# Wider value and state products in the first six chunks, and paired state updates later, in an mLSTM and feed-forward kernel

## The chip, the core and the metric

The kernel runs on one core of one Trainium2 chip. Five engines work side by side and wait for each other through semaphores: TensorE (PE, with its weight loads shown apart as PEld), VectorE (DVE), ScalarE (ACT), GpSimd (POOL) and SyncE (SP), which issues the transfers. The metric is the device time of one execution in microseconds, as the median of several runs. TensorE's clock has two levels, 1.2 and 2.4 GHz; the profile gives the granted one as a share of full speed (1.00 or 0.50).

## What is computed

Four sequences of 768 tokens with 8 heads of 40 channels go through a gated linear recurrence; the result goes through a feed-forward layer with 2048 hidden units. Cut to what matters:

```python
for t in range(S):
    m_new  = maximum(f[t] + m, i[t])
    f_stab = exp(f[t] + m - m_new); i_stab = exp(i[t] - m_new); m = m_new
    C = f_stab * C + i_stab * outer(v[t], k[t])
    n = f_stab * n + i_stab * k[t]
    y[t] = sigmoid(o[t]) * (C @ q[t]) / maximum(abs(n . q[t]), 1)
h = x @ w_in;  out = (maximum(h, 0) + alpha * minimum(h, 0)) @ w_out
```

## The kernel before

**Tiling.** A sequence is cut into 6 chunks of 128 tokens, which makes 24 chunks, numbered n = 0 to 23 over the four sequences; c is a chunk's number in its own sequence. Two chunks make a group of 256 tokens, g = 0 to 11. Inside a chunk the recurrence is done with products: scores `pS` of keys and queries, a decay matrix `E`, their product on DVE (L1082, or L346 later), and then values `pH`: per head the 128x128 matrix E as the stationary operand and the 42 columns of `va` (40 channels, two constants for the denominator) as the moving one. What older chunks left comes from the state C through `pI` (`from_state`). At a chunk's end the state is updated with a product `pu` of the weighed keys `kd` and `va` (`update_steps`); the last chunk of a sequence has no update.

**Two regimes.** The first six chunks (n < NDIR = 6) work with true float32 products (values in `values`, L313 to L326, one 42-column product for each of 8 heads; state in L381, one 84-column product for each of 4 pairs of heads). The trace shows each such float32 product as two matmuls. In that time the weights of the feed-forward layer are loaded and split into a high and a low part (the class `Weights`: ACT, DVE and POOL), which is why all engines are busy there. From n = 6 on all attention products are sums of bf16 parts, but for `pu`, which stays in float32.

**Feed-forward.** Each group runs 8 steps `up` (products `ph`, L742 to L749, 16 of 256 columns a step, in two PSUM banks in turn) and 8 steps `down` (products `po`, L779, 320 columns).

**Order.** The order of the program is a table: ORDER for the first two groups, PATTERN for each later one, in which `ua.0` and `ua.1` are the update products of a group's even and odd chunk. The instructions are pinned to it on each engine, so an instruction that waits holds up all that stand behind it on its engine.

**PSUM.** The attention products share four banks, in two pools "a" and "b" of two buffers, handed out in turn by `psa`.

**Fillers.** `dense` runs products of 256 bf16 columns whose result nobody reads. `values` puts 4, 14 and 4 of them ahead of the value products of chunks 3, 4 and 5 (FILL, L667).

Of the kernel before, what the change touches and what calls it, by code (L numbers as in the profile page):

```python
# [17 lines left out]
def kernel(ctx: ExitStack, tc: tile.TileContext, q, k, v, i_gate, f_gate, o_gate, w_in, w_out, alpha, out):  # L18
# [20 lines left out]
    ps_a = ctx.enter_context(tc.tile_pool(name="ps_a", bufs=2, space=bass.MemoryType.PSUM))  # L39
    turns = ["b", "a"]  # L40

    def psa(name):
        turns.reverse()
        return ps_a.tile([P, 512], F32, tag=turns[0], name=name)


    ident = const.tile([P, P], F32, tag="ident", name="ident")
# [105 lines left out]
        for _ in range(k):  # L153
            nc.tensor.matmul(dst[:, : 2 * P], x[:, :P], x, start=True, stop=True)  # L154

    kds = {}

    def weighed(n):

# [12 lines left out]
    def update_steps(n):  # L172
        b, c = divmod(n, NC)
        if c == NC - 1:
            return
        va = va_t[n // GC % NV][:, n % GC]
        if n not in kds:
            weighed(n)
        kd = kds.pop(n)
        pu = psa(f"pu{n}")  # L180
        pu3 = pu[:, : H * VA].rearrange("p (h e) -> p h e", e=VA)
        for h in range(H):
            r = slice(64 * (h % 2), 64 * (h % 2) + D)
            nc.tensor.matmul(pu3[r, h], kd[:, h], va[:, h], start=True, stop=True)  # L184
        yield
        if b > 0:
            yield from state(n, pu3)
            return
        old, new = C_t[(n - 1) % 3], C_t[n % 3]
        if c > 0 and n in CP:  # L190
            nc.gpsimd.tensor_tensor(
                new[:R], old[:R], gamB[:R, b * H : (b + 1) * H, c : c + 1].broadcast_to([R, H, VA]), ALU.mult
            )
        for par in range(2):
            r = slice(64 * par, 64 * par + D)
            to = by_parity(new[r], par)
            if c == 0:
                nc.vector.tensor_copy(to, by_parity(pu3[r], par))
            else:
                if n not in CP:  # L200
                    gam = gamB[r, b * H + par : (b + 1) * H : 2, c : c + 1].broadcast_to([D, NPR, VA])
                    nc.vector.tensor_tensor(to, by_parity(old[r], par), gam, ALU.mult)
                nc.vector.tensor_tensor(to, to, by_parity(pu3[r], par), ALU.add)
        yield

    def state(n, pu):

        b, c = divmod(n, NC)
        C = C_t[0][:D]
        if c > 0:  # L210
            nc.gpsimd.tensor_tensor(
                C, C, gamB[:D, b * H : (b + 1) * H, c : c + 1].broadcast_to([D, H, VA]), ALU.mult
            )
        yield
        for par in range(2):
            to, new = by_parity(C, par), by_parity(pu[64 * par : 64 * par + D], par)
            if c == 0:
                nc.vector.tensor_copy(to, new)
            else:
                nc.vector.tensor_tensor(to, to, new, ALU.add)  # L220
        yield
        X = state_parts(n)
        C = C.rearrange("p h e -> p (h e)")
        cw = sb.tile([P, 512], F32, tag="qf", name=f"cw{n}")
        rest, high = cw[:D, : H * VA], cw[:D, H * VA :].bitcast(BF16)[:, : H * VA]
        nc.scalar.copy(high, C)
        yield
        nc.gpsimd.tensor_tensor(rest, C, high, ALU.subtract)
        yield
        nc.scalar.copy(X[:D, 0], rest)  # L230
        yield
        nc.gpsimd.tensor_tensor(X[:D, 1], rest, X[:D, 0], ALU.subtract)
        yield
        nc.sync.dma_start(X[D : 2 * D, 0], high)
        nc.sync.dma_start(X[2 * D : 3 * D], high.unsqueeze(1).broadcast_to([D, 2, H * VA]))
        yield
        nc.sync.dma_start(X[D : 2 * D, 1], X[:D, 0])
        yield
# [71 lines left out]
            for _ in value_parts(n):  # L310
                pass

    def values(n, E, busy=lambda: None):  # L313

        pH = psa(f"pH{n}")
        dense(pH, FILL.get(n, 0))
        va = va_t[n // GC % NV][:, n % GC]
        for i in range(H):
            if i % 2 == 0:
                busy()  # L320
            par, p = divmod(i, NPR)
            h = 2 * p + par
            nc.tensor.matmul(  # L323
                pH[:, h * VA : (h + 1) * VA], E[par][:, p * P : (p + 1) * P], va[:, h], start=True, stop=True
            )
        return pH[:, : H * VA].rearrange("p (h e) -> p h e", e=VA)  # L326

# [26 lines left out]
    def values_by_parts(n, Es):  # L354

        V = vbs.pop(n)
        S = sb.tile([P, H, VA], F32, tag="T", name=f"S{n}")
        for par in range(2):
            pH = psa(f"pH{n}_{par}")
            for p in range(NPR):  # L360
                for k, e in enumerate(Es[par]):
                    nc.tensor.matmul(  # L362
                        pH[:, p * 3 * VA : (p * 3 + 3 - k) * VA], e[:, p * P : (p + 1) * P],
                        V[:, 2 * p + par, : 3 - k], start=k == 0, stop=k == 2,
                    )
            yield
            nc.vector.tensor_reduce(
                by_parity(S, par), pH[:, : NPR * 3 * VA].rearrange("p (r k e) -> p r e k", k=3, e=VA),
                mybir.AxisListType.X, ALU.add,
            )  # L370
            yield S

    def from_state(n, qf, Q=None):

        b, c = divmod(n, NC)
        pI = psa(f"pI{n}")
        if b == 0:
            C = C_t[(n - 1) % 3][:R].rearrange("p h e -> p (h e)")
            for p in range(NPR):
                es = slice(2 * p * VA, 2 * (p + 1) * VA)  # L380
                nc.tensor.matmul(pI[:, es], qf[:R, p * P : (p + 1) * P], C[:, es], start=True, stop=True)  # L381
        else:
            C = state_parts(n - 1)[: 3 * D]
            for h in range(H):
                es = slice(h * VA, (h + 1) * VA)
                for s in range(2):
                    nc.tensor.matmul(pI[:, es], Q[: 3 * D, s, h], C[:, s, es], start=s == 0, stop=s == 1)  # L387
        yield
        pI = pI[:, : H * VA].rearrange("p (h e) -> p h e", e=VA)

        T = sb.tile([P, H, VA], F32, tag="T", name=f"T{n}") if n < NBF else pI
        nc.vector.tensor_tensor(T, pI, eT[:, c, b * H : (b + 1) * H].unsqueeze(2).broadcast_to([P, H, VA]), ALU.mult)
        yield T
# [85 lines left out]
    def late_steps(n):  # L479
# [12 lines left out]

        def scores(par):
            Q, K, _ = chunk[n]
            pS[par] = psa(f"pS{n}_{par}")
            for p in range(NPR):
                h = 2 * p + par
                for s in range(2):
                    nc.tensor.matmul(  # L499
                        pS[par][:, p * P : (p + 1) * P], K[: 3 * D, s, h], Q[: 3 * D, s, h], start=s == 0, stop=s == 1  # L500
                    )
            got["s", par] = score_parts(pS[par], E[par], Es[par][2])
# [43 lines left out]
        if n > NDIR:  # L546
            st["sh"] = lambda: shifted(n)
            st["va"] = val
            for k in "bcd":
                st["v" + k] = nxt("v")  # L550
            if c < NC - 1:
                st["wd"] = lambda: weighed(n)
                st["ua"] = upd
                if c > 0:
                    st["ub"] = nxt("u")
                    st["uc"] = nxt("u")
                else:
                    st["uc"] = lambda: (next(got["u"]), next(got["u"]))
                for k in "defghi":
                    st["u" + k] = nxt("u")  # L560
# [79 lines left out]
    def first_stacks():  # L640
# [18 lines left out]
    OFF = 0  # L659
    NDIR = 6  # L660
    NBF = 6
    BEHIND = 4
    XNP = range(2, NBF)
    KDP = range(1, 24)
    CP = range(6, 24)
    OBA = range(0)
    FILL = {3: 4, 4: 14, 5: 4}  # L667
    ORDER = """warm18 kfz alT lf0z warm2 warm2 i00d i00s sca0 lf0a lf0b dq0 L0 sp01 qT0 dq1 alC li0 bj0 wt0 bTt kT0 i00x qc0 kc0 ewj
        i01d sca1 bTc ex01 sp00 sc00 qT1 wTt eeL wTc qc1 wd0 li1 lf1a lf1b kT1 sc01 i00j ex00 kc1 eTt Cz eTc sp11 ex11
        dv0 wg01 i01s wd1 L1 um0 uc0 i01x lpa um1 sp10 wg00 gma gmd ex10 i01j i00h fm1 ft1 sc11 do0 sc10 wg10 bj1 wtl  # L670
# [10 lines left out]
        U12 fm5 ft5 o5h sc51 wg51 v5 o7d R12 S12 ta5 D10 G11 K11 o6s o6x gr5 og3 gg5 G12 gx5 gg4 D11 K12 D12 i30h i30l  # L681
        gx4 U13 gp5 D02 tp0 do3 U06 o7s gp4 o5l o6j vp0 R13 tp1 g05 S13 G13 N05 K13 o7x o6h D13 vp1 o7j U07 tp2 tp3
        R06 S06 R07 x4 x5 xa5 xd5 D03 D04 D05 S07 o7h o7l G06 K06 o6l D06 xa4 xd4 G07 K07 D07 Z0"""
    PATTERN = """og.-1 ua.0 m1.0 V4<< tf.1 ub.0 vb.1 xn.-1 xp.-1 V5<< tg.1 g2<< m0.0 N2<< vc.1 c1.0 r4<< vb.0 d1.0 th.1 h1.0 ti.1 xw.-1 uc.0
        s4<< ud.0 D2<< ue.0 U6<< g4<< l1.0 g3<< N3<< uf.0 r5<< c0.0 vd.1 vc.0 ua.1 sh.1 X:-1 lG.-1 lG.2 ub.1 s5<< N4<<
        R6<< d0.0 g5<< ug.0 h0.0 l0.0 uc.1 V7<< N5<< vd.0 D3<< D4<< D5<< S6<< ta.2 tb.2 xa:-1 uh.0 lL.2
        y0.0 xd:-1 pi.0 r7<< s7<< G6<< wd.2 tc.2 K6<< q0.0 td.2 y1.0 F< q1.0 e0.1 te.2 V0< e1.1 oa.0 tf.2 g7<<
# [261 lines left out]
    def first_group():  # L949
# [38 lines left out]
            nc.vector.tensor_copy(pick[j * BH : (j + 1) * BH], ident[j * BH : (j + 1) * BH, j * BH : (j + 1) * BH])  # L988

        li = row_tile("g_li", "Lb", bufs=2)  # L990
        L = row_tile("g_L", "Lb", bufs=2)
        bj, wj, eL = f, rst, i

        def weights(c0, c1, engine):
# [32 lines left out]
        def spread(n, par):  # L1027

            pb = psa(f"pb{n}_{par}")
            barred(pb)  # L1030
            for p in range(NPR):
                h = 2 * p + par
                nc.tensor.matmul(
                    pb[:, p * P : (p + 1) * P], ident[:BH, h : h + 1].broadcast_to([BH, P]), L[:, n * P : (n + 1) * P],
                    start=False, stop=p == NPR - 1
                )
            rows[n, par] = pb
# [310 lines left out]
```

## Time and profile before

| | |
|---|---|
| median of 3 runs | 470.04 us (470.02 to 470.23) |
| the profiled execution | 470.16 us, of which the span is 468.4 us |
| PE busy | 461.9 us, 99% of the span |
| DVE, ACT, POOL busy | 334.1 us (71%), 316.1 us (67%), 308.4 us (66%) |
| granted TensorE clock | 1.00 but for a stretch of some 10 us from 24.3 us on, at 0.50 |
| PE idle in 40 us stretches from 140 to 420 us | 0.00 us |

The span begins with the first instruction and ends with the last; 1.8 us of the execution lie outside it. A matmul's end is modelled, and neighbours overlap, so a PE that is busy all the time can still be short of its best. How long PE takes for a piece of work is best read from the start of one row to the start of the next. A row of the timeline merges equal instructions that follow each other.

### The profile page before, as it was taken

To read this page: it belongs to the slowest core of one execution; us is meant where nothing else is said; L and a number is where in the kernel's file an instruction comes from. 1 tells how busy PE (TensorE), PEld (TensorE's weight loads), DVE (VectorE), ACT (ScalarE), POOL (GpSimd) and SP (SyncE) were. 2 spreads that over 40 slices of the span, in tenths; PEclk is the share of its full clock that TensorE was granted. 3 is DMA by queue.
4 is the path that set the end of the run, shared out by engine and by line. 5 is a ranking of instruction groups with operands and counts; after the bars stand their busy time and mean duration, and the time that the engine had idled before them with its cause. 6 is when DMAs were issued, how large, how long until landed. Compare 5 with 4: busy or idle time off the path is not lost.

```text
span 468.4 us, 11843 instructions
## 1 busy us (share of the span) xinstructions
PE 461.9 (99%) x4388; PEld 449.2 (96%) x4388; DVE 334.1 (71%) x691; ACT 316.1 (67%) x707; POOL 308.4 (66%) x377
## 2 busy tenths in 40 slices
PE   8999999999999999999999999999999999999996
PEld 6899989999999999999999999999999999999996
DVE  4768988766777887886787887887777886674321
ACT  4969988775857767767867867757857758524331
POOL 8531574864697787597697697587798696324231
PEclk9959999999999999999999999999999999999999
DMA  9988995887786676887996686789895453021000
GB/s 186 197 193 212 233 252 138 192 156 145 154 195 158 129 170 178 134 166 171 160 209 170 121 170 174 146 153 188 172 190 158 96 131 111 1 73 25 29 0 29
DMA packets 186306, 68.68 MB, mean 147 GB/s; under 512 B 150234, under 2 KB 178506, under 8 KB 186250
## 3 DMA queue, kind: packets, MB, share of 16 engines
q1 hardware_dynamic: 186170, 67.83, 66.4%
q8 instruction: 35, 0.57, 0.5%
q14 instruction: 21, 0.17, 0.1%
q10 hardware_dynamic: 80, 0.11, 0.1%
HBM read 40.44 MB, written 7.57 MB: 102 GB/s over the span
## 4 chain that ended last, share of the span: by engine, by line
PE 91%; DVE 5%; ACT 2%; issue 1%; POOL 0%; DVEq 0%; POOLq 0%; ACTq 0%
PE po L779 36%; PE ph L742 5%; PE ph L748 5%; PE ph L745 5%; PE ph L743 5%; PE ph L744 5%; PE ph L747 4%; PE ph L746 4%; PE ph L749 4%; PE pH L362 4%; PE pS L499 3%; PE pH L323 2%; PE pS L1078 2%; PE pu L184 2%; PE pI L387 1%; PE warm L154 1%
## 5 line engine op out<-in xcount | busy, mean ns | idle before, releaser
L768 POOL TENSOR_TENSOR gl<-g,gh 128x512 fp32r<-128x512 f32 x77 | 100.4, 1305 | 43.7 <-ACT gh L766 40.4
L779 PE MATMUL po<-OH,gh 128*128 128x320 f32 x368 | 110.7, 312 | 0.0
L779 PE MATMUL po<-OL,gh 128*128 128x320 f32 x368 | 109.3, 309 | 0.0
L752 ACT ACTIVATE g<-ph 128x512 f32<-128x512 f32 x96 | 57.1, 596 | 58.9 <-PE ph L749 57.7
L757 DVE SCALAR_TENSOR_TENSOR g<-g,oma,ph 128x256 f32<-128x256 f32 x156 | 66.7, 468 | 32.7 <-ACT g L752 32.3
L779 PEld LDWEIGHTS po<-OL,gh 128*128 128x128 f32 x368 | 69.2, 188 | 0.1
L779 PEld LDWEIGHTS po<-OH,gh 128*128 128x128 f32 x368 | 69.1, 188 | 0.0
L779 PE MATMUL po<-OH,gl 128*128 128x320 f32 x368 | 69.0, 309 | 0.0
L742 PE MATMUL ph<-XH,WH 128*128 128x256 f32 x192 | 57.7, 300 | 0.7 <-ACT wo L848 0.7
L779 PEld LDWEIGHTS po<-OH,gl 128*128 128x128 f32 x368 | 58.0, 188 | 0.0
L349 ACT CAST E<-pS 128x512 bf16<-128x512 f32 x72 | 41.7, 582 | 19.2 <-DVE pS L346 15.4
L748 PE MATMUL ph<-XL,WH 128*128 128x256 f32 x192 | 54.3, 283 | 0.0
L745 PE MATMUL ph<-XH,WL 128*128 128x256 f32 x192 | 54.3, 283 | 0.0
L747 PE MATMUL ph<-XL,WH 128*128 128x256 f32 x192 | 54.2, 282 | 0.0
L743 PE MATMUL ph<-XH,WH 128*128 128x256 f32 x192 | 54.1, 282 | 0.0
L744 PE MATMUL ph<-XH,WL 128*128 128x256 f32 x192 | 54.1, 282 | 0.0
L746 PE MATMUL ph<-XH,W 128*128 128x256 f32 x192 | 53.5, 278 | 0.2 <-POOL W L874 0.2
L749 PE MATMUL ph<-XL,W 128*128 128x256 f32 x192 | 53.4, 278 | 0.0
L766 ACT CAST gh<-g 128x512 fp32r<-128x512 f32 x77 | 46.5, 618 | 9.8 <-DVE g L757 7.4
L470 ACT ACTIVATE E<-Lb,bT 128x128 f32<-128x128 f32 x160 | 50.0, 392 | 0.0
L346 DVE TENSOR_TENSOR pS<-pS,E 128x512 f32<-128x512 f32 x36 | 24.7, 690 | 30.7 <-PE pS L499 23.5
L742 PEld LDWEIGHTS ph<-XH,WH 128*128 128x128 f32 x192 | 36.1, 188 | 1.9 <-ACT wo L848 0.9
(197 smaller groups left out, 1144.0 us busy)
## 6 DMA issues: line engine op xcount, KB each, us to landing
Lb<-L_d SPq DMA_DIRECT2D x20, 512.0 KB
wo<-in_moe_w_out_dram SPq DMA_DIRECT2D x8, 640.0 KB
wi<-in_moe_w_in_dram SPq DMA_DIRECT2D x8, 512.0 KB
qn<-in_q_dram SPq DMA_DIRECT2D x24, 160.0 KB
kn<-in_k_dram SPq DMA_DIRECT2D x24, 160.0 KB
va<-in_v_dram SPq DMA_DIRECT2D x24, 160.0 KB
og<-in_o_gate_dram SPq DMA_DIRECT2D x24, 160.0 KB
out_dram<-ob SPq DMA_DIRECT2D x11, 320.0 KB
```

The costliest lines, as they stand in the source:

```text
L742: nc.tensor.matmul(dst, WH[half][:, 0, hs], XH[:, 0], start=True, stop=False)
L743: nc.tensor.matmul(dst, WH[half][:, 1, hs], XH[:, 1], start=False, stop=False)
L744: nc.tensor.matmul(dst, WL[half][:, 0, hs], XH[:, 0], start=False, stop=False)
L745: nc.tensor.matmul(dst, WL[half][:, 1, hs], XH[:, 1], start=False, stop=False)
L746: nc.tensor.matmul(dst, W2[:, fs], X2, start=False, stop=False)
L747: nc.tensor.matmul(dst, WH[half][:, 0, hs], XL[:, 0], start=False, stop=False)
L748: nc.tensor.matmul(dst, WH[half][:, 1, hs], XL[:, 1], start=False, stop=False)
L749: nc.tensor.matmul(dst, W2[:, fs], X2L, start=False, stop=True)
L752: nc.scalar.activation(gt, ph, AF.Relu, scale=-1.0)
L757: nc.vector.scalar_tensor_tensor(out=y[:, e], in0=gt[:, e], scalar=oma[:, f : f + 1], in1=ph[:, e], op0=ALU.mult, op1=ALU.add)
L768: (nc.vector if split else nc.gpsimd).tensor_tensor(gl, y, gh.bitcast(F32), ALU.subtract)
L779: nc.tensor.matmul(po[j], x[:, e, j * P : (j + 1) * P], W[f // NB][:, f % NB], **ends)
```

## The change

Four things are changed.

1. In the first six chunks each value product has 126 columns (WIDE = 3 * VA) in place of 42: the moving operand repeats the head's 42 columns three times, and the result goes to columns that the next heads' products write over. Heads now follow each other as 0, 1, 2, ... in place of 0, 2, 4, 6, 1, 3, 5, 7, so the two E tiles alternate. The state products of chunks 1 to 5 have 126 columns in place of 84, but for the last of the four.
2. The fillers of chunks 3, 4 and 5 are gone.
3. The products that spread the row of decays for chunks 0 and 1 use all 128 rows in place of 32; the rows below are zero, from one more memset on DVE ahead of the first scan.
4. From chunk 7 on the update products of even and odd heads write the same columns in different partitions, so one chunk needs 168 columns of a bank in place of 336. The two chunks of a group then share one bank. From the fifth group on (g > 3) the odd chunk's update is done right behind the even one's (`uA.1` in PATTERN). Five groups have both updates and are moved: 4, 6, 7, 9 and 10. Late tiles get fixed pools: pS "a" and "b" by parity, pI "b", pH and pu "a".

On DVE, ACT, POOL and SP nothing moves; DVE has the memset more.

```diff
@@ psa and its tags
-    def psa(name):
-        turns.reverse()
-        return ps_a.tile([P, 512], F32, tag=turns[0], name=name)
+    def psa(name, tag=None):
+        if tag is None:
+            turns.reverse()
+            tag = turns[0]
+        return ps_a.tile([P, 512], F32, tag=tag, name=name)
+
+    def kept(n, tag, first):
+
+        return tag if n > first else None
...
+    def repeated(ps, at, w):
+
+        return ps[:, at : at + WIDE].rearrange("p (k w) -> p k w", w=w)
@@ update_steps
-        pu = psa(f"pu{n}")
-        pu3 = pu[:, : H * VA].rearrange("p (h e) -> p h e", e=VA)
+        late, j = n > NDIR, n % GC
+        if not late or j == 0 or n - 1 not in pus:
+            pu = psa(f"pu{n}", kept(n, "a", NDIR + 1))
+            if late and j == 0:
+                pus[n] = pu
+        else:
+            pu = pus.pop(n - 1)
+        if late:
+            pu3 = pu[:, j * NPR * VA : (j + 1) * NPR * VA].rearrange("p (r e) -> p r e", e=VA)
+        else:
+            pu3 = pu[:, : H * VA].rearrange("p (h e) -> p h e", e=VA)
         for h in range(H):
             r = slice(64 * (h % 2), 64 * (h % 2) + D)
-            nc.tensor.matmul(pu3[r, h], kd[:, h], va[:, h], start=True, stop=True)
+            nc.tensor.matmul(pu3[r, h // 2 if late else h], kd[:, h], va[:, h], start=True, stop=True)
@@ values
-    def values(n, E, busy=lambda: None):
+    def values(n, E):
 
         pH = psa(f"pH{n}")
-        dense(pH, FILL.get(n, 0))
         va = va_t[n // GC % NV][:, n % GC]
-        for i in range(H):
-            if i % 2 == 0:
-                busy()
-            par, p = divmod(i, NPR)
-            h = 2 * p + par
+        for h in range(H):
             nc.tensor.matmul(
-                pH[:, h * VA : (h + 1) * VA], E[par][:, p * P : (p + 1) * P], va[:, h], start=True, stop=True
+                repeated(pH, h * VA, VA), E[h % 2][:, h // 2 * P : (h // 2 + 1) * P],
+                va[:, h].unsqueeze(1).broadcast_to([P, WIDE // VA, VA]), start=True, stop=True,
             )
@@ from_state
                 es = slice(2 * p * VA, 2 * (p + 1) * VA)
+                es = slice(es.start, min(es.start + WIDE, H * VA))
@@ late_steps and the table
-                st["ua"] = upd
+                st["uA" if j and g > GF else "ua"] = upd
...
-    FILL = {3: 4, 4: 14, 5: 4}
+    WIDE = 3 * VA
...
-    PATTERN = """og.-1 ua.0 m1.0 ...
+    PATTERN = """og.-1 ua.0 uA.1 m1.0 ...
@@ first_group
-        L = row_tile("g_L", "Lb", bufs=2)
+        L_all = sb.tile([P, H, P], F32, tag="Lb", name="g_L", bufs=2).rearrange("p h t -> p (h t)")
+        nc.vector.memset(L_all[:, :GT], 0.0)
+        L = L_all[:BH, :S]
...
-                    pb[:, p * P : (p + 1) * P], ident[:BH, h : h + 1].broadcast_to([BH, P]), L[:, n * P : (n + 1) * P],
+                    pb[:, p * P : (p + 1) * P], ident[:, h : h + 1].broadcast_to([P, P]), L_all[:, n * P : (n + 1) * P],
```

**PE at the values of chunk 5, before.** pI is the state's share, pS_1 the scores of the odd heads, pH the values (first the fillers, four pairs of rows, then four even heads with E_0 and four odd ones with E_1), po the next `down` step.

```order
L381 MATMUL pI_1168<-C_86,qf_874 128x84 x4
L1078 MATMUL pS_1_1176<-qf_874,kf_133 128x128 x4
L154 LDWEIGHTS ident
L154 MATMUL pH_1182<-ident 128x256
...
L323 MATMUL pH_1182<-va_79,E_0_1106 128x42 x4
L323 MATMUL pH_1182<-va_79,E_1_1129 128x42 x4
L779 MATMUL po_0_1039<-OH_104,gg_0_1135 128x320
```

The same place after the change:

```order
L397 MATMUL pI_1151<-C_86,qf_871 128x126 x3
L397 MATMUL pI_1151<-C_86,qf_871 128x84
L1097 MATMUL pS_1_1159<-qf_871,kf_134 128x128 x4
L337 MATMUL pH_1165<-va_79,E_0_1089 128x126
L337 MATMUL pH_1165<-va_79,E_1_1112 128x126
...
L796 MATMUL po_0_1022<-OH_104,gg_0_1118 128x320
```

The fillers are gone, and the first product with E_1 now stands second of eight, not fifth.

**PE at the update products of group 4 (chunks 8 and 9), before.** pS_1 is the end of chunk 8's scores, the first pu row is chunk 8's update, ph_4 to ph_7 are `up` steps of an earlier group; three `up` steps and a `down` step lie between the two updates.

```order
L499 MATMUL pS_1_2045<-qS_1870,kS_1910 128x128
L184 MATMUL pu_2072<-va_79,kd_1717 40x42 x8
L742 MATMUL ph_4_2082<-XH_1418,WH_709 128x256
...
L749 MATMUL ph_6_2160<-XL_1419,W_73 128x256
L184 MATMUL pu_2191<-va_79,kd_1914 40x42 x8
L742 MATMUL ph_7_2224<-XH_1418,WH_709 128x256
```

The same place after the change:

```order
L515 MATMUL pS_1_2024<-qS_1849,kS_1889 128x128
L203 MATMUL pu_2051<-va_79,kd_1696 40x42 x8
L203 MATMUL pu_2051<-va_79,kd_1893 40x42 x8
L759 MATMUL ph_4_2069<-XH_1397,WH_710 128x256
...
L766 MATMUL ph_6_2147<-XL_1398,W_73 128x256
L759 MATMUL ph_7_2202<-XH_1397,WH_710 128x256
```

Chunk 9's eight update products moved up by 60 matmuls, into the bank of chunk 8's, and ph_7 follows ph_6 directly.

## Rows read from the trace of the kernel before

**Rows 1.** Stretches: length; busy us by engine; granted clock; DMA share; GB/s.

```profile
21.00:24.00 3.00, 3.00 (x27) 2.58 (x26) 2.88 (x8) 2.95 (x7) 1.56 (x3) 1.00 0.88 225
24.50:34.50 10.00, 10.00 (x51) 9.19 (x50) 7.01 (x14) 6.10 (x17) 2.35 (x3) 0.50 0.89 181
```

**Rows 2.** Timeline of PE, 18 to 50: start, us, line, out<-in, shapes.

```profile
18.95 1.99 PE L1078 MATMUL pS<-qf,kf 104*128 104x128 f32 x16
...
21.61 1.98 PE L323 MATMUL pH<-va,E 128*128 128x42 f32 x16
...
29.57 0.61 PE L94 MATMUL pb<-later,ident 128*128 128x512 bf16 x1
...
48.36 1.16 PE L1078 MATMUL pS<-qf,kf 104*128 104x128 f32 x8
```

**Rows 3.** Timelines of DVE, ACT, POOL and the SP queue, 27 to 37.

```profile
27.73 0.49 DVE L427 TENSOR_TENSOR xn<-pH,og 128x320 f32<-128x320 f32 x1
...
29.67 0.29 DVE L1007 COPY eT<-ps_ge 128x128 f32<-128x128 f32 x1 [1.45 <-PE ps_ge L1003]
...
32.52 0.69 DVE L1082 TENSOR_TENSOR E<-pS,E 128x512 f32<-128x512 f32 x1 [1.18 <-PE pS L1078]
...
35.39 0.69 DVE L1082 TENSOR_TENSOR E<-pS,E 128x512 f32<-128x512 f32 x1 [1.06 <-PE pS L1078]
...
30.64 1.14 ACT L1061 ACTIVATE E<-pb,bT 128x128 f32<-128x128 f32 x4 [2.82 <-PE pb L1045]
...
35.86 1.40 POOL L162 TENSOR_TENSOR kd<-kn,wT 128x320 f32<-128x320 f32 x2
...
36.60 0.37 SPq L100 DMA_DIRECT2D kn<-in_k_dram  x1
```

**Rows 4.** Stretches, the transfers: length, granted clock, DMA share, GB/s.

```profile
32.00:36.00 4.00, 0.68 0.02 4
...
38.00:52.00 14.00, 1.00 1.07 266
```

**Rows 5.** Chain that ended last, in order of time, 64 to 69.

```profile
64.06 0.81 ACT wo L848
...
68.15 1.53 PE pH L154 x14
```

**Rows 6.** Stretches with busy times, columns as in rows 1.

```profile
70.00:80.00 10.00, 9.98 (x109) 9.57 (x108) 9.58 (x23) 8.22 (x19) 4.45 (x5) 1.00 0.64 157
...
180.00:220.00 40.00, 40.00 (x409) 39.39 (x408) 30.02 (x60) 28.99 (x67) 30.61 (x37) 1.00 0.74 155
```

**Rows 7.** Timeline of PE and of DVE at the values of chunk 5.

```profile
81.14 0.60 PE L154 MATMUL pH<-ident 128*128 128x256 bf16 x4
81.58 1.88 PE L323 MATMUL pH<-va,E 128*128 128x42 f32 x16
83.29 0.39 PE L779 MATMUL po<-OH,gg 128*128 128x320 f32 x1
...
81.42 0.69 DVE L1082 TENSOR_TENSOR E<-pS,E 128x512 f32<-128x512 f32 x1 [0.79 <-POOL E L473]
```

**Rows 8.** Timeline of PE and DVE around updates: chunk 9's, then two together.

```profile
147.00 0.28 PE L749 MATMUL ph<-XL,W 128*128 128x256 f32 x1
147.20 0.51 PE L184 MATMUL pu<-va,kd 128*40 128x42 f32 x16
147.64 0.39 PE L742 MATMUL ph<-XH,WH 128*128 128x256 f32 x1
147.86 0.28 PE L743 MATMUL ph<-XH,WH 128*128 128x256 f32 x1
147.98 0.28 PE L744 MATMUL ph<-XH,WL 128*128 128x256 f32 x1
...
145.95 0.87 DVE L757 SCALAR_TENSOR_TENSOR g<-g,oma,ph 128x256 f32<-128x256 f32 x2 [1.60 <-ACT g L752]
...
73.29 0.81 PE L184 MATMUL pu<-va,kd 128*40 128x42 f32 x32
```

More of the change, by code (lines that the diff above doesn't have):

```diff
@@ L154, in dense @@
             nc.tensor.matmul(dst[:, : 2 * P], x[:, :P], x, start=True, stop=True)
-    kds = {}
+    def repeated(ps, at, w):
+        return ps[:, at : at + WIDE].rearrange("p (k w) -> p k w", w=w)
+    kds, pus = {}, {}
     def weighed(n):
@@ L179, in update_steps @@
         kd = kds.pop(n)
-        pu = psa(f"pu{n}")
-        pu3 = pu[:, : H * VA].rearrange("p (h e) -> p h e", e=VA)
+        late, j = n > NDIR, n % GC
[9 more added lines that the diff above has]
+            pu3 = pu[:, : H * VA].rearrange("p (h e) -> p h e", e=VA)
         for h in range(H):
             r = slice(64 * (h % 2), 64 * (h % 2) + D)
-            nc.tensor.matmul(pu3[r, h], kd[:, h], va[:, h], start=True, stop=True)
+            nc.tensor.matmul(pu3[r, h // 2 if late else h], kd[:, h], va[:, h], start=True, stop=True)
         yield
         if b > 0:
-            yield from state(n, pu3)
+            yield from state(n, [pu3[64 * par : 64 * par + D] if late else by_parity(pu3[64 * par : 64 * par + D], par) for par in range(2)])
             return
@@ L215, in state @@
         for par in range(2):
-            to, new = by_parity(C, par), by_parity(pu[64 * par : 64 * par + D], par)
+            to, new = by_parity(C, par), pu[par]
             if c == 0:
@@ L358, in values_by_parts @@
         for par in range(2):
-            pH = psa(f"pH{n}_{par}")
+            pH = psa(f"pH{n}_{par}", kept(n, "a", NDIR))
             for p in range(NPR):
@@ L375, in from_state @@
         b, c = divmod(n, NC)
-        pI = psa(f"pI{n}")
+        pI = psa(f"pI{n}", kept(n, "b", NDIR))
         if b == 0:
@@ L494, in scores @@
             Q, K, _ = chunk[n]
-            pS[par] = psa(f"pS{n}_{par}")
+            pS[par] = psa(f"pS{n}_{par}", kept(n, "ab"[par], NDIR + 1))
             for p in range(NPR):
@@ L661 @@
     NBF = 6
+    GF = NDIR // GC
     BEHIND = 4
@@ L683 @@
         R06 S06 R07 x4 x5 xa5 xd5 D03 D04 D05 S07 o7h o7l G06 K06 o6l D06 xa4 xd4 G07 K07 D07 Z0"""
-    PATTERN = """og.-1 ua.0 m1.0 V4<< tf.1 ub.0 vb.1 xn.-1 xp.-1 V5<< tg.1 g2<< m0.0 N2<< vc.1 c1.0 r4<< vb.0 d1.0 th.1 h1.0 ti.1 xw.-1 uc.0
+    PATTERN = """og.-1 ua.0 uA.1 m1.0 V4<< tf.1 ub.0 vb.1 xn.-1 xp.-1 V5<< tg.1 g2<< m0.0 N2<< vc.1 c1.0 r4<< vb.0 d1.0 th.1 h1.0 ti.1 xw.-1 uc.0
         s4<< ud.0 D2<< ue.0 U6<< g4<< l1.0 g3<< N3<< uf.0 r5<< c0.0 vd.1 vc.0 ua.1 sh.1 X:-1 lG.-1 lG.2 ub.1 s5<< N4<<
```

## The prediction

> **What bounds the kernel now.** I read the stretches first. From 140 us on PE is busy all the time and nobody makes it wait; the row of 180 to 220 stands for six such stretches [rows 6]. What PE does there is the time, so an instruction less on PE counts in full. The start is different: ACT and DVE convert the weights while the first chunks run, and the chain goes through them, as at 64.06 [rows 5]. And there is a stretch in which PE itself is slow: from about 24.5 to 34.5 us the granted clock is 0.50, which is the 1.2 GHz level, and before it 1.00 [rows 1]. PE never idled ahead of the fall: it was busy for 3.00 of 3.00 us. What it did was 16 matmuls of 42 columns, with transposes and some small products around them [rows 1, 2]. So I look for three things in the rows: what PE's slow stretch costs, which of the fillers lie on a path, and what an update product costs PE where PE is the bound.
>
> **The change part by part.**
>
> *The clock (part 1, and its cost).* At full clock 16 matmuls of 128 columns take 1.99 us and 16 of 42 columns 1.98 us [rows 2]: the moving columns are not what such a float32 product is paid for. So 126 columns cost between nothing and what the slowest case of 128 columns shows, 8 in 1.16 us, which is 2.32 for 16 against 1.98: up to 0.34 us a chunk [rows 2]. I take 0.1, since the direct comparison is nearest. The state products go from 84 to 126 columns; by the same rows that is nothing. Here a page speaks against the change. The Trainium skill, "TensorE: Matmul & The Clock Gate", section "Back-to-back issue gap", makes a stream of matmuls cost its columns; by it 84 more columns at 2.4 GHz are 35 ns a matmul, an estimate of 0.6 us a chunk, and 0.6 us later where a chunk's values end on the path. The rows disagree with it for these float32 products.
>
> For the clock itself I expect that it holds at 24.3: the stretch before the fall then has three times the moving columns in its 16 value matmuls, and the scores at 18.95, as wide as that, ran at full clock and kept it [rows 2]. PE's 10 us at half clock would be 5 us. How much of the other 5 arrives is a matter of who is late next. The first hold is the product at 29.57: it writes the bank of chunk 0's values, which DVE frees with xn, 27.73 + 0.49 = 28.22 [rows 2, 3]. So it starts at 28.3, 1.3 us earlier. From its start to ACT's exponentials are 1.07 us at half clock, 0.54 at full; the exponentials take 1.14, so DVE multiplies at 28.3 + 0.54 + 1.14 = 30.0 in place of 32.52: 2.5 us earlier [rows 2, 3]. DVE itself is in time for it: its small work from 29.67 to 31.34 (32.52 less the idle 1.18) is 1.67 us, its idle 1.45 ahead of that was for PE, so the work can run from 28.22 to 29.9. On this multiplication hang xn of chunk 1, the POOL work up to kd, and SP's load of kn at 36.60, which waits for kd: all 2.5 us earlier. From 32.52 to 35.39 DVE idles 1.06 for PE and works 1.81; with PE ahead the second multiplication comes at 30.0 + 1.8 = 31.8, 3.6 us earlier [rows 3]. So two offsets enter the conversion stage: 3.6 us for PE, DVE and ACT, 2.5 us for the loads. The loads matter: the transfer engines stand still from 32 to 36, because SP waits for kd, and are full from 38 to 52 [rows 3, 4]. No view shows how long a load lies ready before its use, so the stage comes out between 2.5 and 3.6 us earlier. I take 3.0, in the middle, with 2.4 to 3.8 as ends.
>
> *The fillers (part 2).* Chunk 4's fourteen are on the chain with 1.53 us [rows 5]. But DVE is busy for 9.58 of the next 10 us [rows 6], in its own order, so it takes up at most 0.42 us of that before it holds PE again. I take 0 and keep 0.4 for the range. Chunk 3's four stand inside the conversion stage and are covered by ACT and DVE there. Without this cover they would be worth a little over 0.4 us, as chunk 5's are. Chunk 5's four take 81.58 - 81.14 = 0.44 us of PE, and here the new order of heads bites. The values needed E of the odd heads from their fifth product on; now the second needs it. That E comes from DVE at 81.42 + 0.69 = 82.11, held by POOL [rows 7]. Now eight products run from 81.58 to 83.29, 0.214 us each. After the change the first runs at 81.14, PE then waits until 82.1, and seven more take 1.5 us, or 1.6 to 1.8 with the price of columns: the end is 83.6 to 83.9 against 83.29. So this place loses 0.3 to 0.6 us, and I take 0.4. Behind PE's wait stand the `down` products of group 1, which are PE's bound from there on.
>
> *The spread over 128 rows and the memset (part 3).* The same number of matmuls with the same columns. DVE's memset stands ahead of a scan that waits for the gates to arrive; that wait covers it. Were it not covered it would be one pass of DVE over 256 columns, about half of a 0.69 us row [rows 3]. I take 0.
>
> *The paired updates (part 4).* An update between two `up` steps: from the last ph before it (147.00) to the second ph behind it (147.86) are 0.86 us, where two ordinary steps are 2 x 0.12 = 0.24 (147.98 - 147.86 is one). So it costs 0.62 us. Two updates together are a row of 0.81 us, one is a row of 0.51, so the second costs 0.30 [rows 8]. Moving it saves 0.32 us, in five groups 1.6 us, all of it in the stretch where PE is the bound. What could take it back is the next step's bank: ph_7 needs DVE's work on ph_5, done at 145.95 + 0.87 = 146.82, and starts at 147.64: 0.82 us of slack [rows 8]. ph_7 then comes 0.32 earlier and ph_5 0.30 later, so 0.2 is left and no wait follows. The shared bank is read by DVE only after both updates, and the weighed keys of the odd chunk are made a group's part earlier on POOL; if they were late PE would wait at the earlier place with all of ph behind it. For the range: 0.2 to 0.4 a group, 1.0 to 2.0 us.
>
> *Sum.* Against the profiled execution, 470.16 us: -3.0 (clock) + 0.4 (chunk 5) - 1.6 (updates) = -4.2, so 465.96. The median of the runs is 0.12 lower, 470.04, which gives 465.8. With all ends: -3.8 - 0.4 + 0.3 - 2.0 = -5.9 and -2.4 + 0.6 - 1.0 = -2.8, so 464.1 to 467.2.
>
> **The rivals.**
>
> *A. The wide products do not hold the clock, and only the known fall stays.* For it: PE was not idle before the fall, so what brought it is not seen in idle time [rows 1]. Then only the updates and chunk 5 are left: 470.0 - 1.6 + 0.4 = 468.8. The Trainium skill, "TensorE: Matmul & The Clock Gate", section "Why this matters for your kernels", names idle gaps of TensorE as what loses the clock; by that alone nothing changes here, because there was no gap to close, and the time is this rival's. The trace does not bear the rule out, as the clock fell without a gap.
>
> *B. The conversion stage keeps most of the gain.* The transfer engines are full from 38 to 52 [rows 4] and ACT and DVE nearly so; if loads arrive just when they are used, and run no faster when they start earlier, only 1 to 1.5 us come through: 470.0 - 1.2 + 0.4 - 1.6 = 467.6. Against it: the idle time of 32 to 36 is on the transfer engines as well.
>
> *C. Slower: the fillers were what held the clock at chunks 4 and 5.* If wide products do not replace them, the clock falls at 24.3 as before and again after chunk 5, where PE is the bound and nothing else hides it. Ten us of slow clock as in rows 1 cost up to 5 us there: 468.8 + 5 = 473.8; with half of it 471.3. It decides from the point at which the granted clock shows 0.50 anywhere after 60 us for more than about 2.5 us.
>
> **How the numbers follow.** The forecast has a chance of 0.76, A 0.06, B 0.13, C 0.05. The range holds the forecast and most of B: 464.2 to 467.9. A measurement of this kernel tells about 0.2% from no change, that is 0.94 us: faster means below 469.1. The forecast and B are faster; of A, at 468.8, I count two thirds as faster and the rest as the same, and half of C's weaker cases as the same. Faster 0.92, same 0.04, slower 0.04.
>
> **What would show it.** Right: a granted clock of 1.00 from 20 to 40; the first E multiplication of chunk 2 near 30 and kn's load near 34; PE's transposes of x near 31.5; the chain through ACT at 64.06 now near 61; a wait of PE on DVE inside chunk 5's values of nearly 0.8 us; update pairs of 0.74 us and ph_7 straight behind ph_6 without a wait. Wrong: a stretch at 0.50 between 20 and 100; value matmuls of 126 columns at more than 0.145 us each; PE idle for long near 62 to 65, which would mean that the weights, not PE, set the stage; PE waiting for ph banks in the five moved groups.

## The result and the profile after

The changed kernel takes 465.1 us (median of four executions, 464.7 to 465.35) beside 470.13 us before (470.02 to 470.24): a ratio of 0.9896, interval 0.9881 to 0.991. The forecast was 465.8. Repeated twice, the ratio was 0.9918 (0.989 to 0.9946) and 0.9913 (0.9885 to 0.9942), with 464.57 and 464.59 us for the changed kernel. In those repeats the kernel before varied from one execution to the next, and that this goes with its granted clock is the main thing the experiments found.

The profiled execution of after is 465.35 us with a span of 463.6, against 470.16 and 468.4. The stretches, columns as in [rows 1]:

```profile
21.00:24.00 3.00, 2.63 (x24) 2.24 (x23) 2.49 (x10) 2.39 (x5) 0.20 (x1) 1.00 0.82 125
24.50:34.50 10.00, 8.43 (x75) 7.23 (x73) 8.98 (x18) 9.13 (x23) 5.37 (x7) 1.00 0.97 219
32.00:36.00 4.00, 3.67 (x43) 3.18 (x44) 3.33 (x8) 3.61 (x10) 2.71 (x4) 1.00 0.37 55
38.00:52.00 14.00, 13.82 (x132) 13.22 (x131) 13.24 (x30) 13.78 (x30) 4.29 (x4) 1.00 1.08 273
```

The granted clock is 1.00 where [rows 1] show 0.50. PE is no longer busy all the time there (8.43 of 10 us): it is ahead and waits. The transfer engines work from 32 to 36 us (0.37 against 0.02 in [rows 4]).

PE, DVE and the SP queue in that part, timeline of after, which answers [rows 2, 3]:

```profile
17.80 1.99 PE L1097 MATMUL pS<-qf,kf 104*128 104x128 f32 x16
20.47 2.05 PE L337 MATMUL pH<-va,E 128*128 128x126 f32 x16
28.05 0.38 PE L100 MATMUL pb<-later,ident 128*128 128x512 bf16 x1 [0.84 <-DVE xn L443]
27.51 0.49 DVE L443 TENSOR_TENSOR xn<-pH,og 128x320 f32<-128x320 f32 x1
30.13 0.69 DVE L1101 TENSOR_TENSOR E<-pS,E 128x512 f32<-128x512 f32 x1 [0.55 <-PE pb L1064]
31.97 0.69 DVE L1101 TENSOR_TENSOR E<-pS,E 128x512 f32<-128x512 f32 x1
34.22 0.37 SPq L106 DMA_DIRECT2D kn<-in_k_dram  x1
```

Sixteen matmuls of 126 columns take 2.05 us, 0.07 more than of 42. The bar of chunk 2 at 28.05 waits for xn, the hold that the prediction named. The two multiplications are 2.4 and 3.4 us earlier than before, the load of kn 2.4.

The chain of waits of after, start and length, further on:

```profile
28.56 4.91 DMA qn<-in_q_dram
...
37.39 8.24 DMA wi<-in_moe_w_in_dram
...
60.39 0.80 ACT wo L865
61.25 0.36 PE ph L759
```

ACT's wo is 3.67 us earlier than in [rows 5], so the conversion stage passed on all that PE had gained. Not all of it is the clock's: PE began the scores 1.15 us earlier (17.80 against 18.95 in [rows 2]) before the place of the fall. The wait for xn at 28.05 took up most of that lead, as xn itself came only 0.22 us earlier (27.51 against 27.73). The chain now goes through two loads, where before it held no transfer between 28 and 72 us.

Chunk 5's values, timeline of PE and DVE, which answers [rows 7]:

```profile
77.47 0.39 PE L337 MATMUL pH<-va,E 128*128 128x126 f32 x2
78.49 1.83 PE L337 MATMUL pH<-va,E 128*128 128x126 f32 x14 [0.63 <-DVE E L1101]
80.07 0.39 PE L796 MATMUL po<-OH,gg 128*128 128x320 f32 x1
77.74 0.69 DVE L1101 TENSOR_TENSOR E<-pS,E 128x512 f32<-128x512 f32 x1 [0.80 <-POOL E L489]
```

One head runs, PE waits for the odd heads' E, seven follow. From entering to `down` it is 2.60 us against 83.29 - 81.14 = 2.15 before [rows 7]: 0.45 lost.

The paired updates of group 4 and the steps behind them (timeline of PE, after), which answer [rows 8]:

```profile
135.93 0.81 PE L203 MATMUL pu<-va,kd 128*40 128x42 f32 x32
136.67 0.39 PE L759 MATMUL ph<-XH,WH 128*128 128x256 f32 x1
...
144.09 0.28 PE L766 MATMUL ph<-XL,W 128*128 128x256 f32 x1
144.20 0.28 PE L759 MATMUL ph<-XH,WH 128*128 128x256 f32 x1
```

A pair costs 0.74 us, and ph_7 follows ph_6 after 0.11 us. PE waits for nobody from 130 to 420 us. The first values product of chunk 7 and that of chunk 23 stand on either side of the five moved updates. Before, then after (timelines of PE):

```profile
133.59 1.10 PE L362 MATMUL pH<-vb,E 128*128 128x126 bf16 x24
...
412.83 1.04 PE L362 MATMUL pH<-vb,E 128*128 128x126 bf16 x22
```

```profile
130.37 1.10 PE L377 MATMUL pH<-vb,E 128*128 128x126 bf16 x24
...
408.01 1.08 PE L377 MATMUL pH<-vb,E 128*128 128x126 bf16 x23
```

3.22 us earlier at chunk 7, 4.82 at chunk 23: 1.60 us for five updates.

### The profile page after: what moved, and what is told of

Its sections match the earlier page's. It is cut to its first block, busy times and chain, and to the rows that moved or that the text cites. A ratio compares the mean times of both kernels' runs of the same rounds, so it can differ in the third digit from the quotient of the medians.

```text
span 463.6 us, 11813 instructions
## 1 busy us (share of the span) xinstructions
PE 452.8 (98%) x4366; PEld 442.0 (95%) x4366; DVE 329.8 (71%) x692; ACT 315.0 (68%) x707; POOL 308.4 (67%) x377
## 4 chain that ended last, share of the span: by engine, by line
PE 83%; DVE 5%; DMA 5%; SPq 3%; ACT 3%; issue 1%; ACTq 0%; DVEq 0%
PE po L796 36%; PE ph L759 5%; PE ph L765 5%; PE ph L762 5%; PE ph L760 5%; PE ph L761 5%; PE ph L764 4%; PE ph L763 4%; PE ph L766 4%; PE pH L377 4%; PE pS L515 4%; DMA wi<-in_moe_w_in_dram 2%; DMA wr<-in_moe_w_in_dram 2%; PE pI L403 1%; PE pu L203 1%; DMA qn<-in_q_dram 1%
```

## The experiments

Each kernel ran beside the kernel before on one chip, four kernels to a chip. Intervals of differences are 95%, of the medians, by resampling the executions. The first four gave 23 executions of before, the next four 30, the last four 21. "Clock" is the mean granted clock of an execution, lowest to highest.

| kernel | executions | median us | lowest to highest | clock |
|---|---|---|---|---|
| before, three chips | 74 | 467.84 | 465.65 to 470.64 | 0.988 to 1.000 |
| after, first comparison and two repeats | 21 | 464.68 | 463.70 to 466.57 | 0.998 to 1.000 |
| after, 42 columns, no fillers | 12 | 467.76 | 465.98 to 471.36 | 0.982 to 0.996 |
| the same with fillers | 12 | 467.03 | 463.73 to 468.43 | 0.988 to 1.000 |
| after, 84 columns | 12 | 465.12 | 464.43 to 467.83 | 0.995 to 1.000 |
| after, 84 columns for the state alone | 8 | 465.03 | 464.56 to 466.05 | 0.999 to 1.000 |
| before with part 1 alone | 12 | 466.48 | 466.07 to 467.91 | 0.998 to 1.000 |
| after, spread over 32 rows | 10 | 465.20 | 464.71 to 465.79 | 0.999 to 1.000 |
| after, updates not moved | 12 | 466.54 | 466.01 to 467.94 | 0.999 to 1.000 |
| after, chunk 4's fillers back | 6 | 464.67 | 464.39 to 465.00 | 0.999 to 1.000 |
| after, chunk 5's even heads first (twice) | 6 + 6 | 464.51, 464.71 | 463.87 to 465.76 | 0.998 to 1.000 |

### The clock: 42 columns, without fillers and with them

```diff
-    WIDE = 3 * VA
+    WIDE = VA
...
-                es = slice(es.start, min(es.start + WIDE, H * VA))
+                es = slice(es.start, es.start + 2 * VA)
```

> The changed kernel with 42 columns a value product and 84 a state product again, still without fillers. My theory: the 126 columns are what holds the clock, so the granted clock falls to 0.50 near 24 us again and the time goes back by the 3.0 to 3.7 us that came from it: 468.1 to 468.8. Rival 1 (something else in the change holds the clock, the spread over 128 rows or the earlier start): clock 1.00 throughout, 465.1. Rival 2 (fillers held the clock at chunks 4 and 5): a second fall after 60 us, 470 or more.

The clock fell in all twelve executions (0.996 at best). The stretches of the profiled one, columns as in [rows 1]:

```profile
27.00:31.00 4.00, 3.76 (x21) 3.25 (x21) 2.17 (x7) 1.94 (x7) 0.24 (x1) 0.57 1.21 250
...
61.00:65.00 4.00, 4.00 (x20) 3.86 (x21) 3.78 (x7) 3.96 (x7) 3.18 (x5) 0.57 0.71 137
...
82.00:89.00 7.00, 7.00 (x30) 7.00 (x30) 4.25 (x10) 3.48 (x6) 3.28 (x5) 0.51 0.82 207
```

Three falls: one behind chunk 1's values, one in the conversion stage ahead of chunk 4's, one during chunk 5's. So the first rival, that something else holds the clock, is out. The second one holds as well as my theory: the late falls are rival C of the prediction, and without the wide products they are real. This execution took 471.36 us, the longest of the twelve. In the others the clock was lost in varying amounts, and the median of 467.76 is only a little under the 468.1 to 468.8 expected.

The next run puts the fillers back at 42 columns:

```diff
         pH = psa(f"pH{n}")
+        dense(pH, {3: 4, 4: 14, 5: 4}.get(n, 0))
```

> The changed kernel with 42 and 84 columns as in the first experiment, but with the fillers of chunks 3, 4 and 5 back: parts 3 and 4 alone, with the heads in plain order. It tells what the fillers did. My theory: they hold the clock at chunks 4 and 5, and only the narrow products of chunks 0 and 1 let it fall, so the clock is 0.988 to 1.000 as in the kernel before and never 0.982 to 0.985 as without fillers; times from 464.3 (466.15 of the executions of before without a fall - 1.6 - 0.6 + 0.3) to 468.2 (470.07 less the same), a median of 466. Rival (the fillers did nothing for the clock): clocks down to 0.982 and a median of 467.8 as in the first experiment.

```profile
27.00:31.00 4.00, 3.67 (x21) 3.06 (x21) 2.09 (x7) 2.33 (x8) 0.24 (x1) 0.57 1.18 251
...
61.00:89.00 28.00, 26.93 (x243) 25.94 (x242) 23.15 (x47) 22.12 (x47) 16.81 (x21) 1.00 0.79 190
```

The early fall is there, the two late ones are gone, and no execution is under 0.988, where five of twelve were without fillers. So the fillers did hold the clock later on; the profile shows that for one execution, the lowest mean clocks bear it out for the others. The clock fell in eleven of twelve. The times (463.73 to 468.43) reach a little beyond both ends of what I expected; the median, 467.03, is 1 us higher than expected, with falls in all but one execution.

### How many columns, and in which products

84 columns:

```diff
-    WIDE = 3 * VA
+    WIDE = 2 * VA
```

> The changed kernel with 84 columns a product for values and state, without fillers. With 42 the clock fell in every execution (0.982 to 0.996), with 126 in none. If columns are what counts, 84 lies between: I expect falls in part of the executions, a median of 465.5 to 467. Rival (any repeat will do): 0.998 or more each time and 465.1.

Ten of twelve executions held the clock, two had 0.995 and 0.996. So falls in part of them came true, but fewer than I reckoned: the median, 465.12, lies under the 465.5 to 467 expected. 84 columns nearly do; with 126 for the values no fall was seen in 81 executions. Wide values with the state products as they were:

```diff
-                es = slice(es.start, min(es.start + WIDE, H * VA))
+                es = slice(es.start, es.start + 2 * VA)
```

> The changed kernel with 126 columns for the values and 84 for the state products. My theory: the values, 16 matmuls in a row, are what counts, so the clock stays at 0.998 or more and the time is its partner's, 464.6. Rival (the state products are needed too): clocks below 0.997 in part of the executions and a median over 465.5.

The clock held in all eight. The median is 0.44 us above its partner's (after, on the same chip: 464.59), with an interval of -0.22 to 0.98 that holds zero. So the values are what counts, and the wider state products have no effect that these runs can tell.

### Part 1 alone on the kernel before

```diff
-            par, p = divmod(i, NPR)
-            h = 2 * p + par
             nc.tensor.matmul(
-                pH[:, h * VA : (h + 1) * VA], E[par][:, p * P : (p + 1) * P], va[:, h], start=True, stop=True
+                repeated(pH, h * VA, VA), E[h % 2][:, h // 2 * P : (h // 2 + 1) * P],
+                va[:, h].unsqueeze(1).broadcast_to([P, WIDE // VA, VA]), start=True, stop=True,
             )
```

> The kernel before with part 1 alone: 126 columns and the heads in plain order, but its fillers, its 32-row spread and its update places. My theory: the columns alone hold the clock, so the granted clock is 0.998 or more in every execution. The time is then that of the executions of before in which the clock did not fall (465.9 to 467.2) plus 0.3 for the wait on the odd heads' E in chunk 5 behind the fillers: 466.2 to 467.5. Rival (the 128 rows of the spread are needed too): clocks down to 0.988, and 470 in part of the executions.

0.998 or more in all twelve: part 1 alone is enough. It also changes the order of the heads, but the two runs with 42 columns kept that order and fell, so it is the columns. 466.48 is 0.30 above the 466.18 of the executions of before in which the clock held, the price expected for the head order in chunk 5, though its interval (-0.15 to 0.77) holds zero. In the profile this place takes 79.74 - 77.14 = 2.60 us, 0.45 more than in [rows 7].

### Part 3 undone: the spread over 32 rows

```diff
-        L_all = sb.tile([P, H, P], F32, tag="Lb", name="g_L", bufs=2).rearrange("p h t -> p (h t)")
-        nc.vector.memset(L_all[:, :GT], 0.0)
-        L = L_all[:BH, :S]
+        L = row_tile("g_L", "Lb", bufs=2)
...
-                    pb[:, ...], ident[:, h : h + 1].broadcast_to([P, P]), L_all[:, n * P : (n + 1) * P],
+                    pb[:, ...], ident[:BH, h : h + 1].broadcast_to([BH, P]), L[:, n * P : (n + 1) * P],
```

> The changed kernel with the spread over 32 rows again (part 3 undone). In the trace of after the step from the bar to the spread's products takes 0.23 us in place of 0.32, and the spread with the next product 0.98 in place of 1.08: 0.2 us for each of four spreads, 0.8 us in all. My theory: PE reaches chunk 0's values 0.8 us later and the clock holds; the end comes 0 to 0.8 us later, since the loads do not start earlier by it: 465.1 to 465.9, I take 465.5. Rival 1 (the spread holds the clock): clocks below 0.997 in part of the executions and 467 to 470. Rival 2 (nothing): 465.1.

The clock held, so the first rival is out. The end is 0.63 us later than the changed kernel on the same chip (interval 0.11 to 0.91), so the second is out too. PE in the second pair of spreads with 32 rows:

```profile
14.16 0.39 PE L100 MATMUL pb<-later,ident 128*128 128x512 bf16 x1
14.48 1.15 PE L1050 MATMUL pb<-g_L,ident 32*128 32x128 f32 x8
15.56 0.81 PE L203 MATMUL pu<-va,kd 128*40 128x42 f32 x32
...
18.67 1.99 PE L1095 MATMUL pS<-qf,kf 104*128 104x128 f32 x16
```

and with 128 rows, in the kernel with the updates not moved, whose profile began much the same:

```profile
14.07 0.39 PE L100 MATMUL pb<-later,ident 128*128 128x512 bf16 x1
14.29 1.05 PE L1052 MATMUL pb<-g_L,ident 128*128 128x128 f32 x8
15.28 0.81 PE L203 MATMUL pu<-va,kd 128*40 128x42 f32 x32
...
18.00 1.99 PE L1097 MATMUL pS<-qf,kf 104*128 104x128 f32 x16
```

From bar to spread 0.32 against 0.22, from spread to `pu` 1.08 against 0.99, and from the first bar to the scores 4.51 against 3.93. The eight products themselves are as many with as many columns; what is saved is going from 128 rows to 32 and back. The weight loads of this spread show the first of these steps (timeline of PEld, 32 rows, then 128):

```profile
14.48 0.96 PEld L1050 LDWEIGHTS pb<-g_L,ident 32*128 32x128 f32 x8 [0.23 <-issue]
```

```profile
14.07 1.09 PEld L1052 LDWEIGHTS pb<-g_L,ident 128*128 128x128 f32 x8
```

With 128 rows the first load starts as the bar does, at 14.07; with 32 rows the loads stand still for 0.23 us and start with the products, at 14.48.

These profiles also show when the gain arrives. PE waits for xn at chunk 2's bar in all of them (0.84 to 0.93 us where the clock held). The bar starts at 27.98 here and at 27.89 in part 1 alone, both with 32 rows. With 128 rows it starts between 27.21 and 27.43 in five profiles, and between 27.73 and 28.05 in four in which the transposes of chunk 2's queries begin 0.2 to 0.6 us late behind the values; in three of these PE is seen waiting for the load. One of the four is the first profile of after, so there part 3 can have given next to nothing. The 0.63 us of the medians (0.52, interval 0.08 to 0.81, against all 21 executions of after) is best read as a mixture of executions with the gain and without it; that was not tested by itself.

### Updates not moved

```diff
-                st["uA" if j and g > GF else "ua"] = upd
+                st["uA" if j and g > NG else "ua"] = upd
```

> The changed kernel with the odd chunk's update back at its old place in all groups, the shared banks kept. My theory: each of the five moved updates is worth 0.32 us, so 465.1 + 1.6 = 466.7. Rival (the fixed pools and shared banks, not the place, gave it): 465.1.

466.54, 0.2 under my figure. Against the pooled executions of after it is 1.86 us longer (interval 1.35 to 2.52), which holds the 1.60 of the rows. In the profiles, from chunk 5's first `down` product to the last copy of the output are 460.96 - 79.33 = 381.63 us, against 460.12 - 80.07 = 380.05 in after: 1.58. The place gives it, not the shared bank.

### Chunk 4's fillers back

```diff
         pH = psa(f"pH{n}")
+        dense(pH, 14 if n == 4 else 0)
```

> The changed kernel with the fourteen fillers ahead of chunk 4's values back. My theory: DVE is busy for 9.6 of 10 us behind them, so they cost at most 0.4 us: 465.1 to 465.5. Rival (they lay on the path in full, and DVE's queue gives way): 1.5 us, 466.6.

No cost. PE with the fillers, from the transposes of keys ahead of chunk 4's values to chunk 5's scores:

```profile
63.54 0.60 PE L266 MATMUL pqk<-ident,kn 128*104 128x128 f32 x4
63.98 1.69 PE L160 MATMUL pH<-ident 128*128 128x256 bf16 x14
...
76.13 1.16 PE L1098 MATMUL pS<-qf,kf 104*128 104x128 f32 x8
```

and the changed kernel itself (second profile):

```profile
63.04 0.60 PE L266 MATMUL pqk<-ident,kn 128*104 128x128 f32 x4
...
75.64 1.16 PE L1097 MATMUL pS<-qf,kf 104*128 104x128 f32 x8
```

0.50 us apart ahead of the 1.5 us of fillers, 0.49 apart behind: they are free there.

### Chunk 5's even heads first

```diff
-        for h in range(H):
+        for i in range(H):
+            h = 2 * (i % NPR) + i // NPR if n == 5 else i
             nc.tensor.matmul(
-                repeated(pH, h * VA, VA), ...
+                repeated(pH, i * VA, VA), ...
```

(The sum with the state's share reads the result in that order.)

> The changed kernel, but chunk 5's value products run the four even heads first again (their 126 columns laid out in the order of running). My theory: PE's wait of 0.8 us for the odd heads' E inside these products goes, and with it the 0.4 to 0.5 us that this place lost: 464.6, at best 464.3. Rival (the next instruction on PE waits in its place): 465.1.

```profile
76.96 2.17 PE L338 MATMUL pH<-va,E 128*128 128x126 f32 x16
78.89 0.40 PE L799 MATMUL po<-OH,gg 128*128 128x320 f32 x1
```

The wait is gone: 1.93 us in place of 2.60. The median was 464.51, with no partner on its chip, so it ran again beside the changed kernel, which also gave two repeats of that one:

> The changed kernel itself once more, beside the kernel before and the parts below. In the first four experiments the kernel before had a granted clock of 0.988 to 1.000 from one execution to the next, and 470.0 to 470.2 us only where it was lowest; the three kernels with 126 columns had 0.998 or more each time. My theory: the same here, so the changed kernel stays at 464.7 to 465.8 in every execution, and the kernel before spreads from 465.9 to 470.2, so that the two medians lie 2 to 5 us apart. Rival (that chip was peculiar): the kernel before at 470.1 each time.

> The kernel of the third experiment once more (chunk 5's even heads first), now beside the changed kernel. In its first profile the place that costs the changed kernel 0.45 us gave 0.13 instead. My theory: 0.5 us below its partner, 464.1. Rival (the gain is lost behind chunk 5 or is no larger than the spread of the loads): within 0.2 us of its partner.

> The changed kernel a third time, as the partner on this chip of the next one: 464.6, clock 0.998 or more each time.

The clock of the changed kernel came out as expected both times. Its times were lower than expected in the first repeat, six of nine under 464.7 and down to 463.70, and one execution in each was long (466.57 and 466.28). The even heads first were 0.12 us slower than their partner (interval -0.81 to 0.64); all executions of both kernels pooled, 0.09 faster (-0.56 to 0.25). So the rival's 0.2 us is what the times say. The profiles settle where the 0.67 us of the place go: from chunk 5's first `down` product to the last copy of the output are 380.15 and 380.14 us with the even heads first, against 380.03 to 380.11 in the three profiles of the changed kernel. Nothing behind the place takes the gain back. The times don't show it because the stage ahead of the place varies by more than that from one execution to the next (last section), so by its times this version can't be called better.

## Why the prediction came out, and where it did not

**The clock.** The kind is right: 126 columns hold it, shown from both sides (part 1 alone holds it, 42 columns in the changed kernel let it fall). The places are right too: 28.05 for the bar (28.3 predicted), 30.13 for the first multiplication (30.0), 34.22 for kn (near 34), 31.97 for the second (31.8), ACT's chain near 61. The term was mis-sized in two ways. I took 3.0 us, halfway between the offset of the loads (2.5) and that of PE (3.6). All of PE's offset came through, 3.67 at ACT's wo. The loads are now on the chain, as I feared, but the chain of before held none there, so they had time to spare and their 2.4 us were enough. The kernel before says the same by itself: its 30 executions with a clock of 0.988 or 0.989 have a median of 470.12, its 18 with 0.998 or more 466.18. The fall costs 3.9 us (interval 3.4 to 4.2). In the two profiles it is less: 3.67 less the 0.22 by which xn came earlier leaves some 3.4 us, an estimate.

The other fault is that I took the fall for part of the kernel. It came in 470.02 to 470.24 us four times in the first comparison, which gave no sign that it could stay away. In the experiments, 18 of 74 executions had none, 22 had a clock of 0.995 or 0.996 (median 467.45), four 0.992 or 0.993, 30 the full one. So the change saves nothing of this term in a quarter of the executions, and 3.9 us in two fifths. Its median gain is 3.2 us (467.84 to 464.68), where the first comparison shows 5.0.

**Part 3.** This term was missed: I took 0, because the number of products and their columns said the same price, and it measured 0.63 us (interval 0.11 to 0.91). I had priced the products and not the change between 128 and 32 rows ahead of and behind them, though the trace of before shows the same 0.32 us from the bar to the spread as the 32-row timeline above. The Trainium skill, "TensorE: Matmul & The Clock Gate", section "LDWEIGHTS (loading the stationary operand)", says that a weight load of 32 rows takes as long as one of 128. For the load by itself the traces agree: the spread's loads have a median of 185 ns with 32 rows and of 191 with 128. By that alone part 3 would be worth nothing, but the timelines above show some 0.1 us at each passage between the two, which that section doesn't treat.

**Fillers.** Chunk 4's: taken as 0, measured 0. Chunk 5's place: 0.4 lost predicted, 0.45 lost in the rows, by the named wait (0.63 us, not 0.8: one head was running).

**Updates.** Five times 0.32 us, 1.6 in all: exact in the rows, and inside the interval of the run that undoes it. No wait for banks followed: PE was busy all the time from 130 to 420 us.

**Columns.** 0.07 us a chunk against 0.1 taken. The prediction weighed a rule against this, from the Trainium skill, "TensorE: Matmul & The Clock Gate", section "Back-to-back issue gap": an estimate of 0.6 us, which the rows do not bear out. The prediction read the section too narrowly: it gives that formula for a matmul by itself and says that in a stream in which each matmul has its weight load the two together set the spacing. The value products are such a stream: 96 matmuls with 96 loads in the trace of after.

**The sum by what was measured.** Between the two profiled executions PE came to chunk 5's values (before: to the fillers ahead of them) 81.14 - 77.47 = 3.67 us earlier, 0.45 was lost there and the updates gave 1.6: 4.8 us, which is 470.16 - 465.35. So the forecast of 465.8 was 0.7 high in the first comparison because the early stage gave 3.67 in place of 3.0, in a profile in which part 3 can have given next to nothing (see above). By the medians the terms are -3.9 + 0.45 - 0.63 - 1.6 = -5.7, so 470.12 - 5.7 = 464.4, against 464.68; the 0.3 between them is less than the width of the terms' intervals. Against executions of before that held their clock the change is worth 1.5 us (466.18 to 464.68, interval 1.1 to 1.9).

**Rivals.** A is out (part 1 alone holds the clock). B is out: where it let 1 to 1.5 us through, ACT's wo came 3.67 us earlier. C named something real: without fillers and without width the clock does fall after 60 us. The width prevents it.

## What to carry over

A granted clock that falls in one profiled execution may stay up in the next; take the mean clock of many executions before pricing it, and compare those with and without the fall. When costing a product, price the passages to its neighbours as well: a change of row count between neighbouring products had a price of its own. A wait removed from a place that the steady part follows is worth its rows, but a stage that varies by more hides it from the time.

## What the runs showed of the hardware

**The fall is a matter of the execution, not of the program alone.** The same program held the clock in 18 of 74 executions. The rise at the start also moves. The four warm products ahead of the first spread, in the profiles of before and of after:

```profile
5.59 1.03 PE L154 MATMUL warm<-ident 128*128 128x256 bf16 x4
```

```profile
5.25 0.61 PE L160 MATMUL warm<-ident 128*128 128x256 bf16 x4
```

The second ran at full clock already. On PE the change has nothing ahead of them, and other profiles of changed kernels have 1.03 there. The Trainium skill, "TensorE: Matmul & The Clock Gate", section "What's actually happening", says that the window of the monitor behind the clock runs freely and does not restart with the kernel. It says so of the rise, and the two rows above fit it; that the fall varies for the same reason is not shown. An early rise did not make the end earlier: the profile of the unmoved updates has 1.03 there and is 0.75 us ahead of after at chunk 4's values (63.56 against 64.31).

**A load's landing sets the early stage.** With the clock held, chunk 4's values start between 63.5 and 64.4 us in the profiles of kernels with 126 columns and no fillers. In the profile of after PE waits for chunk 2's queries:

```profile
22.89 0.29 PE L266 MATMUL pqk<-ident,qn 128*104 128x128 f32 x1 [0.37 <-DMA qn<-in_q_dram]
```

The second profile of the same kernel has no such wait and reaches chunk 4's values at 63.48; its wi load is issued 0.9 us earlier (chain of waits):

```profile
36.48 8.36 DMA wi<-in_moe_w_in_dram
```

So in these executions the loads, not PE, are late next in this stage. Issuing wi ahead of kn, which waits for POOL's kd, would be the next thing to try; it was not tried. The rare long executions at full clock (466.57, 466.53) may come from there too: one was profiled, with 84 columns, and its chain runs through a load of the row of decays that took 12.56 us.

```profile
38.25 12.56 DMA Lb<-L_d
...
50.83 1.28 ACT E L486 x4
```

Why columns and fillers decide whether the clock falls stays open; the runs show only which products decide it. Idle time alone does not: in the kernel before the clock fell behind 3.00 us of 3.00 in which PE was busy [rows 1], and in the changed kernel it held although PE was busy for only 2.63 of those 3.00 us and 8.43 of the 10 that followed.
